# Attention's first pair of heads: one head prepared alone, the other in the first slot, with one rotation table

## The chip, the cores and the metric

The kernel runs on one core of one Trainium2 chip. A core has TensorE (PE in the views, its weight loads PEld), VectorE (DVE), ScalarE (ACT), GpSimd (POOL) and SyncE (SP), each with an instruction stream of its own that it works off in order; they wait for each other by semaphores. Data come from HBM by DMAs that are issued on a queue of an engine, here mostly SyncE's. The metric is the time of one execution on the device in microseconds, the median over several runs; lower is better.

## What is computed

```python
def _attn_ref(q, k, v):                      # (2, 8, 576, 64), f32
    def rotate(x):
        x1, x2 = (x[..., :half], x[..., half:])
        return np.concatenate([x1 * cos - x2 * sin, x1 * sin + x2 * cos], axis=-1)
    q_rot, k_rot = (rotate(q), rotate(k))
    scores = scale * np.matmul(q_rot, k_rot.transpose(0, 1, 3, 2))
    scores = scores - np.max(scores, axis=-1, keepdims=True)
    attn = np.exp(scores)
    attn = attn / (np.sum(attn, axis=-1, keepdims=True) + 1e-09)
    return np.matmul(attn, v)

def reference(...):
    x = attn_out.transpose(0, 2, 1, 3).reshape(B * S, H * D)
    x = _moe_ref(x=x, ...)       # soft mixture: 8 experts, every token through each
    return _moe2_ref(x=x, ...)   # hard mixture: a greedy assignment, 144 tokens an expert
```

Sixteen (batch, head) attentions are followed by two mixtures of experts. The change touches the start of attention alone.

## The kernel before

Attention works head after head, g = 0 to 15, two heads to a pair P. A head's rotated q and k are split into a high and a low part (`hl`, the high part rounded to the matmul's f32r format and the low part what is left), so that products keep f32 accuracy. The order of every instruction is written out by hand: each engine gets its instructions in the order in which the Python code calls them. In the loop over g (a slot for each head) the calls are collected by `at(t, f, ...)` and sorted by t, a position within the slot from 0 to 5; the table `SC` holds most positions.

Before the first slot the first pair is prepared, both heads together:

- `load` (L1127) issues for each of k, q, v three DMAs on SyncE's queue: 128 KB for each of the two heads, then 32 KB that hold the last 64 rows of both (the rest load). The tiles `rawk`, `rawq`, `rawv` are single, so the next pair's load waits until the rotation has read them. ScalarE's queue loads the rotation table `tab` in two parts of 320 KB: part 1 for k, part 0, which is part 1 scaled by 1/8, for q.
- `prep_rot` (L1176) rotates: two cross products into scratch (L1185, L1186), a product with the cosine into `t1k` or `t1q` (L1188), and the sum (L1189). For the first pair VectorE does all of k and L1188 and L1189 of q; for later pairs GpSimd does everything. `t1k` and `t1q` are single tiles.
- `prep_hl` (L1192) makes the parts: the high part on ScalarE (L1201), the low part (L1202) on VectorE for the first pair and on GpSimd later. k needs each part twice. For the first pair ScalarE and VectorE compute the second copy (L1207, L1208); later pairs get it by two DMAs inside SBUF, on SyncE's queue, 320 KB each (L1204 the high part, L1205 the low).
- `tq` (L1224) transposes a head's parts on TensorE into one PSUM bank at a time (u = 0 high k, 1 low k, 2 q, 3 the last 64 rows), and VectorE or ScalarE move them to `khh`, `kll`, `qs`. `score` (L1254) multiplies them, VectorE takes the maximum (L1264), ScalarE the exponential (L1268). `te` (L1272) transposes the exponentials, ScalarE and VectorE split them into `ah` and `al` (L1295, L1303), `pv` (L1309) multiplies with v. `prep_v` (L1210) splits v on GpSimd, two operations.
- `warm` (L1159) issues matmuls of zeros that nothing reads; the seven counts in `WARM` say how many stand at which place.

The transposes of head g+2 stand ahead of their slot: `tq(2, 0)`, the first that needs the second pair's k, stands at position 3.21 of slot 0, `tq(2, 1)` at 0.8 of slot 1, `tq(2, 2)` at 2.12 of slot 1. TensorE works in order, so whatever one of them waits for holds up all that follows.

Of the kernel before, what the change touches and what calls it, by code (L numbers as in the profile page):

```python
# [1109 lines left out]
def attention(tc, nc, ps, pss, lp, q, k, v, rope, ident, xH, xL, m1):  # L1110
    with ExitStack() as st:
# [13 lines left out]

        def load(P, names):
            if P >= B * NH // 2:  # L1127
                return
            b, pr = divmod(P, 4)
            for n in names:  # L1130
                src = SRC[n]
                t = raw[n][P % NR]
                off = (b * NH + 2 * pr) * S * HD
                for h in range(2):
                    nc.sync.dma_start(
                        t[:, h, 0:4, :].rearrange("p (t r) d -> p t (r d)", r=2),
                        bass.AP(tensor=src.tensor, offset=src.offset + off + h * S * HD,
                                ap=[[2 * HD, 128], [256 * HD, 2], [1, 2 * HD]]))
                nc.sync.dma_start(
                    t[0:64, :, 4, :],  # L1140
                    bass.AP(tensor=src.tensor, offset=src.offset + off + 512 * HD,
                            ap=[[HD, 64], [S * HD, 2], [1, HD]]))
# [33 lines left out]
        def prep_rot(P, n):  # L1176
            e1 = nc.vector if P == 0 and n == "k" else nc.gpsimd
            e2 = nc.gpsimd if P else nc.vector
            x = raw[n][P % NR]
# [1 line left out]
            cos = tab[:, ti, :, 0:64].unsqueeze(1).to_broadcast([128, 2, 5, 64])
            nsin = tab[:, ti, :, 64:96].unsqueeze(1).to_broadcast([128, 2, 5, 32])
            sin = tab[:, ti, :, 96:128].unsqueeze(1).to_broadcast([128, 2, 5, 32])
            t2 = pone.tile([128, 2, 5, HD], F32, name="t2")
            e1.tensor_tensor(t2[:, :, :, 0:32], x[:, :, :, 32:64], nsin, op=OP.mult)  # L1185
# [340 lines left out]
```

## Time and profile before

| what | value |
| --- | --- |
| time, median of 3 runs | 1189.12 us (1187.91 to 1190.19) |
| the profiled execution: its time | 1186.11 us |
| its span, first to last instruction | 1184.3 us |
| TensorE busy | 1151.8 us, 97% of the span |
| VectorE, ScalarE, GpSimd busy | 788.0, 415.8, 475.8 us |
| mean granted clock of TensorE | 0.991 of full |

The span is cut into 40 slices on the profile's page; the first, up to 29.6 us, is where the change lies. TensorE is busy for seven tenths of it and for nine tenths of most later ones. Busy time says little about the start, where TensorE also works off warm-up matmuls: there the timelines of single engines are read, an instruction a line, and the order of the instructions beside them.

### The profile page before, as it was taken

What the parts mean: (1) busy time and instruction counts of PE and PEld (TensorE: products, weight loads), DVE (VectorE), ACT (ScalarE), POOL (GpSimd) and SP (SyncE); (2) the same over time, 40 slices, a digit from 0 to 9 for tenths busy, and PEclk for the clock granted to TensorE, in tenths of its full rate; (3) what the DMA queues carried; (4) which work ended last, traced back from release to release, by engine and by line L of the source; (5) the groups of instructions that cost most, each with busy time, mean ns of one, the idle gap of its engine ahead of it and who ended that gap; (6) DMA issues with size and microseconds to landing.
All of it is one profiled execution on the core that took longest, in us unless ns stands there. A gap on an engine that the chain in (4) does not pass through costs nothing. (4 is left out here: it accounts for less than half of the span.)

```text
span 1184.3 us, 19903 instructions
## 1 busy us (share of the span) xinstructions
PE 1151.8 (97%) x7743; PEld 1036.9 (88%) x7743; DVE 788.0 (67%) x1710; ACT 415.8 (35%) x934; POOL 475.8 (40%) x428
## 2 busy tenths in 40 slices
PE   7999999999899999999999999999999999899997
PEld 4988988898798989898889898988988887899997
DVE  6999995255666666666666666548798768789200
ACT  4888886214333232323232323231121120222222
POOL 6787855405454335433543454151040000364111
PEclk8999999999899999999999999999999999999999
DMA  3223214200121112111211121142000003878830
GB/s 105 73 71 88 53 33 149 72 1 1 36 58 50 36 37 69 39 37 36 69 39 36 37 72 36 36 178 72 1 36 1 27 1 125 285 265 291 269 102 20
DMA packets 92766, 90.07 MB, mean 76 GB/s; under 512 B 26369, under 2 KB 65409, under 8 KB 92545
## 3 DMA queue, kind: packets, MB, share of 16 engines
q1 hardware_dynamic: 90336, 83.43, 22.4%
q0 software_dynamic: 2048, 4.72, 1.3%
q8 instruction: 61, 1.00, 0.4%
q10 hardware_dynamic: 288, 0.66, 0.2%
q14 instruction: 33, 0.26, 0.1%
HBM read 79.48 MB, written 4.72 MB: 71 GB/s over the span
## 5 line engine op out<-in xcount | busy, mean ns | idle before, releaser
L874 DVE TENSOR_TENSOR v<-T,v 128x256 f32<-128x256 f32 (+1 forms) x200 | 90.6, 453 | 75.9 <-PE T L861 74.6
L921 DVE SCALAR_TENSOR_TENSOR acc<-Y,pw,acc 128x512 f32<-128x512 f32 x180 | 132.3, 744 | 5.4 <-PE Y L919 2.6
L682 PE MATMUL T<-xH,wa 128*128 128x384 f32 x480 | 132.4, 337 | 0.0
L861 PE MATMUL T<-xH,wa 128*128 128x256 f32 (+1 forms) x480 | 115.4, 296 | 0.0
L861 PEld LDWEIGHTS T<-big,wb 128*128 128x128 f32 x720 | 104.4, 188 | 10.3 <-DVE v L874 3.3
L861 PE MATMUL T<-big,wb 128*128 128x256 f32 (+1 forms) x720 | 108.4, 294 | 3.1 <-DVE v L874 3.1
L701 PE MATMUL Y<-wb,hh 128*128 128x512 f32 x312 | 98.2, 396 | 1.6 <-ACT acc L708 1.6
L690 ACT ACTIVATE hh<-T 128x384 fp32r<-128x384 f32 x62 | 30.5, 492 | 185.4 <-PE T L682 185.2
L682 PEld LDWEIGHTS T<-xH,wa 128*128 128x128 f32 x480 | 87.6, 188 | 2.9
L861 PEld LDWEIGHTS T<-xH,wa 128*128 128x128 f32 x480 | 84.4, 190 | 5.1
L691 DVE SCALAR_TENSOR_TENSOR hl<-T,hh 128x384 fp32r<-128x384 f32 x62 | 34.5, 556 | 78.1 <-ACT hh L690 78.0
L682 PE MATMUL T<-xL,wa 128*128 128x384 f32 x240 | 80.6, 336 | 0.0
L861 PE MATMUL T<-xL,wa 128*128 128x256 f32 (+1 forms) x240 | 71.0, 296 | 0.0
L868 DVE SCALAR_TENSOR_TENSOR hlB<-v,hhB 128x320 fp32r<-128x320 f32 x60 | 47.4, 791 | 32.3 <-ACT hhB L867 32.3
L770 POOL TENSOR_TENSOR wa<-wraw,wa 128x512 fp32r<-128x512 f32 (+1 forms) x40 | 41.0, 1025 | 64.7 <-ACT wa L769 64.7
L701 PEld LDWEIGHTS Y<-wb,hh 128*128 128x128 f32 x312 | 57.1, 188 | 11.3 <-ACT acc L708 2.1
L789 POOL TENSOR_TENSOR wb<-wraw,wb 128x512 fp32r<-128x512 f32 x20 | 25.5, 1296 | 99.8 <-ACT wb L788 99.8
L867 ACT ACTIVATE hhB<-v 128x320 fp32r<-128x320 f32 x60 | 28.3, 472 | 104.2 <-DVE v L874 104.2
L789 POOL TENSOR_TENSOR wa<-wraw,wa 128x512 fp32r<-128x512 f32 x20 | 25.9, 1318 | 96.2 <-ACT wa L788 96.2
L1264 DVE TENSOR_REDUCE negmax<-S 128x1 f32<-128x576 f32 (+1 forms) x80 | 60.1, 752 | 5.5 <-PE S L1262 4.7
L919 PE MATMUL Y<-wa,hhB 128*128 128x512 f32 x200 | 62.9, 396 | 0.0
L919 PE MATMUL Y<-wb,hhB 128*128 128x512 f32 x200 | 62.8, 396 | 0.0
(292 smaller groups left out, 3041.8 us busy)
## 6 DMA issues: line engine op xcount, KB each, us to landing
wraw<-in_moe_w SPq DMA_DIRECT2D x56, 512.0 KB, 5.0
big<-in_moe_w SPq DMA_DIRECT2D x22, 512.0 KB, 6.3
wraw<-in_moe_w SPq DMA_DIRECT2D x40, 256.0 KB, 3.2
wa<-in_moe_w SPq DMA_DIRECT2D x18, 512.0 KB, 5.1
wb<-in_moe_w SPq DMA_DIRECT2D x12, 512.0 KB, 5.9
hlk<-hlk SPq DMA_DIRECT2D x14, 320.0 KB, 3.4
ysc<-acc SPq DMA_DIRECT2D x9, 256.0 KB, 2.1
rawk<-in_k SPq DMA_DIRECT2D x16, 128.0 KB, 3.9
```

What stands on the lines that cost most here:

```text
L682: nc.tensor.matmul(p[:, :CH], w[:, wi, kt, (fb % 2) * 128:(fb % 2) * 128 + 128], x[:, kt, o], start=(n == 0), stop=(n == 11))
L690: nc.scalar.activation(hh, p[:, :CH], AF.Relu)
L691: nc.vector.scalar_tensor_tensor(hl, p[:, :CH], 0.0, hh.bitcast(F32), op0=OP.max, op1=OP.subtract)
L701: nc.tensor.matmul(self.Y[c][t], a[:, o], w[:, wi, fb % 2], start=(fb == 0 and n == 0), stop=(fb == FB - 1 and n == 2))
L770: G.tensor_tensor(l, src, h.bitcast(F32), op=OP.subtract)
L789: G.tensor_tensor(d["W"][:, 1, h], r[:, 2 + h], d["W"][:, 0, h].bitcast(F32), op=OP.subtract)
L861: nc.tensor.matmul(bank[:, 0:n], d[t][:, ww, b, r * 128:(r + 1) * 128], x(xw, r), start=(first and i == 0), stop=(i == 5), skip_group_chec ...
L868: V.scalar_tensor_tensor(HL[:, f, o], src, 0.0, HH[:, f, o].bitcast(F32), op0=OP.max, op1=OP.subtract)
L874: V.tensor_tensor(o, bank[:, 0:n], x, op=OP.add)
L919: nc.tensor.matmul(y, h[:, f, o], w[:, ww, f], start=(f == 0 and z == 0), stop=(f == 1 and z == 2))
L921: V.scalar_tensor_tensor(self.acc[:, t], y, self.pw[:, t, e:e + 1], self.acc[:, t], op0=OP.mult, op1=OP.add)
L1264: nc.vector.tensor_reduce(m[0:n], p[0:n, :, :288], axis=AX.XY, op=OP.max, negate=True)
```

## The change

Only head 0 of the first pair is loaded first (k, its rest, q, its rest), rotated and split before the first slot; head 1 follows inside slot 0. k's first head is rotated on VectorE, q's first head and k's second head on GpSimd, q's second head on VectorE in slot 0. The scratch tile is one for k and one for q. One rotation table is loaded; ScalarE computes the scaled one from it. The rotation of the next pair's k and q moves into slot 0, behind the first pair's second head and on either side of `prep_v`; its `prep_hl` moves from positions 0.9 (k) and 2.9 (q) of slot 0 to 3.1 of slot 0 and 1.6 of slot 1; the load of pair 2's k and q moves from 0.9 to 3.1. `tq(1, 0)` and `tq(1, 1)` move from positions 0.01 and 0.02 to 2.05 and 2.06; `tq(1, 2)` and `tq(1, 3)` stay at 2.12 and 2.16. The counts of warm-up matmuls at the first three places go from 8, 6, 3 to 16, 3, 2.

```diff
-        WARM = (8, 6, 3, 4, 3, 2, 2)
+        WARM = (16, 3, 2, 4, 3, 2, 2)
...
-        load(0, "k")
-        nc.scalar.dma_start(tab[:, 1], rope[:, 1])
-        load(0, "q")
-        nc.scalar.dma_start(tab[:, 0], rope[:, 0])
+        nc.scalar.dma_start(tab[:, 1], rope)
+        for n in "kq":
+            load_h(0, n, 0)
+            load_r(0, n)
+        for n in "kq":
+            load_h(0, n, 1)
         load(0, "v")
+        nc.scalar.activation(tab[:, 0], tab[:, 1], AF.Copy, scale=0.125)
...
-        def prep_rot(P, n):
-            e1 = nc.vector if P == 0 and n == "k" else nc.gpsimd
-            e2 = nc.gpsimd if P else nc.vector
-            x = raw[n][P % NR]
+        def prep_rot(P, n, h=None, e=nc.gpsimd):
+            hs = slice(0, 2) if h is None else slice(h, h + 1)
+            nh = hs.stop - hs.start
+            x = raw[n][P % NR][:, hs]
...
-            t2 = pone.tile([128, 2, 5, HD], F32, name="t2")
+            t2 = pone.tile([128, 2, 5, HD], F32, name="t2" + n)[:, hs]
...
+            if not h:
+                T1[n, P] = pone.tile([128, 2, 5, HD], F32, name="t1" + n)
+            t1 = T1[n, P][:, hs]
+            e.tensor_tensor(t1, x, cos, op=OP.mult)
+            e.tensor_tensor(t1, t1, t2, op=OP.add)
...
-        prep_rot(0, "k")
-        prep_rot(0, "q")
-        load(1, "kq")
-        prep_hl(0, "k")
-        prep_hl(0, "q")
+        prep_rot(0, "k", 0, nc.vector)
+        prep_rot(0, "q", 0)
+        prep_hl(0, "k", 0)
+        prep_rot(0, "k", 1)
+        load(1, "k")
+        prep_hl(0, "q", 0)
...
-        prep_rot(1, "k")
-        prep_rot(1, "q")
...
-                        at(SC["tqs"] + 0.01 * u, tq, 1, u)
+                        at(2.05 + 0.01 * u, tq, 1, u)
...
-                at(0.9, prep_hl, 1, "k")
-                at(0.9, load, 2, "kq")
+                at(0.02, prep_rot, 0, "q", 1, nc.vector)
+                at(0.02, load, 1, "q")
+                at(0.9, prep_hl, 0, "k", 1)
+                at(0.91, prep_rot, 1, "k")
+                at(1.3, prep_hl, 0, "q", 1)
                 at(1.9, prep_v, 0)
                 at(1.9, load, 1, "v")
-                at(2.9, prep_hl, 1, "q")
+                at(1.92, prep_rot, 1, "q")
+                at(3.1, prep_hl, 1, "k")
+                at(3.1, load, 2, "kq")
+            if g == 1:
+                at(1.6, prep_hl, 1, "q")
```

`prep_hl` gets the same parameter h. The host makes one table instead of two. The lines of the changed kernel lie some 10 to 15 higher: L1196, L1197, L1201, L1202 are the four operations of a rotation, L1216 and L1222 the low parts, L1228 and L1229 `prep_v`, L1130 and L1139 the loads, L1218 and L1219 the two copies.

GpSimd, from the rotation of the second pair's k on; before (big_113 is the split v, the names with numbers are scratch):

```order
L1185 TENSOR_TENSOR t_207<-rawk_96,tab 128x10x32 [waits DMAHW4_49,DMAHW3_49,DMAHW5_49,DMAHW0_49,DVE_49]
L1186 TENSOR_TENSOR t_207<-rawk_96,tab 128x10x32
L1188 TENSOR_TENSOR t1k<-rawk_96,tab 128x640 [waits DVE_49]
L1189 TENSOR_TENSOR t1k<-t1k,t_207 128x640 [waits Pool_49]
L1185 TENSOR_TENSOR t_213<-rawq_95,tab 128x10x32 [waits DMAHW6_49,DMAHW7_49,DMAHW0_49,Pool_49]
L1186 TENSOR_TENSOR t_213<-rawq_95,tab 128x10x32
L1188 TENSOR_TENSOR t1q<-rawq_95,tab 128x640 [waits DVE_49]
L1189 TENSOR_TENSOR t1q<-t1q,t_213 128x640 [waits Pool_49]
L1202 TENSOR_TENSOR hlk<-t1k,hlk 128x10x64 [waits Activation_49]
L1214 TENSOR_TENSOR big_113<-rawv_97,zero 128x2x5x64 [waits DMAHW2_49,DMAHW1_49]
L1215 TENSOR_TENSOR big_113<-rawv_97,big_113 128x2x5x64 [waits Pool_49]
L1202 TENSOR_TENSOR hlq<-t1q,hlq 128x10x64 [waits Activation_49]
```

The same place in the changed kernel, from the last operation on the first pair's second k head:

```order
L1202 TENSOR_TENSOR t1k<-t1k,t2k 128x320 [waits Pool_49]
L1196 TENSOR_TENSOR t2k<-rawk_96,tab 128x10x32 [waits DMAHW3_49,DMAHW4_49,DMAHW2_49,Pool_49]
L1197 TENSOR_TENSOR t2k<-rawk_96,tab 128x10x32
L1201 TENSOR_TENSOR t1k<-rawk_96,tab 128x640 [waits DVE_49]
L1202 TENSOR_TENSOR t1k<-t1k,t2k 128x640 [waits Pool_49]
L1228 TENSOR_TENSOR big_113<-rawv_97,zero 128x2x5x64 [waits DMAHW7_49,DMAHW1_49,DMAHW0_49]
L1229 TENSOR_TENSOR big_113<-rawv_97,big_113 128x2x5x64 [waits Pool_49]
L1196 TENSOR_TENSOR t2q<-rawq_95,tab 128x10x32 [waits DMAHW7_49,DMAHW6_49,DMAHW5_49]
L1197 TENSOR_TENSOR t2q<-rawq_95,tab 128x10x32
L1201 TENSOR_TENSOR t1q<-rawq_95,tab 128x640 [waits DVE_49]
L1202 TENSOR_TENSOR t1q<-t1q,t2q 128x640 [waits Pool_49]
L1216 TENSOR_TENSOR hlk<-t1k,hlk 128x10x64 [waits Activation_49]
```

The split of v has come ahead of q's rotation and q's rotation ahead of k's low part, and the third operation of k's rotation has a wait for VectorE.

SyncE's queue, from the second pair's k load on; before:

```order
L1135 DMA rawk_96<-in_k 128x2x128 [waits DMAHW3_49,DVE_49]
L1135 DMA rawk_96<-in_k 128x2x128 [waits DMAHW4_49]
L1139 DMA rawk_96<-in_k 64x2x64 [waits DMAHW5_49]
L1135 DMA rawq_95<-in_q 128x2x128 [waits DMAHW6_49,DVE_49,Pool_49]
L1135 DMA rawq_95<-in_q 128x2x128 [waits DMAHW7_49]
L1139 DMA rawq_95<-in_q 64x2x64 [waits DMAHW0_49]
L1204 DMA hlk<-hlk 128x10x64 [waits DMAHW1_49,Activation_49]
L1205 DMA hlk<-hlk 128x10x64 [waits DMAHW2_49,Pool_49]
L1135 DMA rawk_96<-in_k 128x2x128 [waits DMAHW3_49]
L1135 DMA rawk_96<-in_k 128x2x128 [waits DMAHW4_49]
L1139 DMA rawk_96<-in_k 64x2x64 [waits DMAHW5_49]
L1135 DMA rawq_95<-in_q 128x2x128 [waits DMAHW6_49]
```

And in the changed kernel:

```order
L1130 DMA rawk_96<-in_k 128x2x128 [waits DMAHW2_49,DVE_49]
L1130 DMA rawk_96<-in_k 128x2x128 [waits DMAHW5_49,DMAHW3_49,Pool_49]
L1139 DMA rawk_96<-in_k 64x2x64 [waits DMAHW4_49]
L1130 DMA rawq_95<-in_q 128x2x128
L1130 DMA rawq_95<-in_q 128x2x128 [waits DMAHW6_49,DVE_49]
L1139 DMA rawq_95<-in_q 64x2x64 [waits DMAHW7_49]
L1130 DMA rawv_97<-in_v 128x2x128 [waits DMAHW0_49,Pool_49]
L1130 DMA rawv_97<-in_v 128x2x128 [waits DMAHW1_49]
L1139 DMA rawv_97<-in_v 64x2x64 [waits DMAHW2_49]
L1218 DMA hlk<-hlk 128x10x64 [waits DMAHW3_49,Activation_49]
L1219 DMA hlk<-hlk 128x10x64 [waits DMAHW4_49,Pool_49]
```

The second pair's v load, which stood behind the two hlk copies and the third pair's loads, stands ahead of the copies, with its wait for GpSimd.

VectorE, from the first pair's low parts to the first low part of weights (al); before:

```order
L1202 TENSOR_TENSOR hlk<-t1k,hlk 128x10x64 [waits Activation_49]
L1208 TENSOR_TENSOR hlk<-t1k,hlk 128x10x64 [waits Activation_49]
L1202 TENSOR_TENSOR hlq<-t1q,hlq 128x10x64 [waits Activation_49]
L1244 CAST khh<-T 128x512 [waits PE_49]
L1244 CAST kll<-T 128x512 [waits PE_49]
L1251 CAST kll<-T 128x64 [waits Activation_49]
L1264 TENSOR_REDUCE negmax<-S 128x1 [waits PE_49] x2
L1244 CAST khh<-T 128x512 [waits PE_49]
L1244 CAST kll<-T 128x512 [waits PE_49]
L1264 TENSOR_REDUCE negmax<-S 128x1 [waits PE_49]
L1303 SCALAR_TENSOR_TENSOR al<-T,ah 128x4x128 [waits Activation_49]
```

In the changed kernel, from the first two maxima on:

```order
L1278 TENSOR_REDUCE negmax<-S 128x1 [waits PE_49] x2
L1196 TENSOR_TENSOR t2q<-rawq_95,tab 128x5x32 [waits DMAHW6_49,DMAHW4_49]
L1197 TENSOR_TENSOR t2q<-rawq_95,tab 128x5x32
L1201 TENSOR_TENSOR t1q<-rawq_95,tab 128x320
L1202 TENSOR_TENSOR t1q<-t1q,t2q 128x320 [waits DVE_49]
L1278 TENSOR_REDUCE negmax<-S 128x1 [waits PE_49]
L1317 SCALAR_TENSOR_TENSOR al<-T,ah 128x4x128 [waits Activation_49]
L1216 TENSOR_TENSOR hlk<-t1k,hlk 128x5x64 [waits Activation_49]
L1222 TENSOR_TENSOR hlk<-t1k,hlk 128x5x64 [waits Activation_49]
L1278 TENSOR_REDUCE negmax<-S 128x1 [waits PE_49]
L1317 SCALAR_TENSOR_TENSOR al<-T,ah 128x4x128 [waits Activation_49]
L1216 TENSOR_TENSOR hlq<-t1q,hlq 128x5x64 [waits DVE_49,Activation_49]
```

q's second head is rotated between the second and the third maximum, and three half low parts stand behind the scores instead of in front of them.

## Rows read from the trace of the kernel before

**Rows 1.** Stage table: stretch, length, busy us (count) of each engine, PEclk, DMA, GB/s

```profile
1.27:4.90 3.63, 3.59 (x8) 1.01 (x8) 0.47 (x7) 1.28 (x1) 0.54 (x4) 1.00 0.81 245
...
8.00:9.00 1.00, 0.00 (x0) 0.00 (x0) 0.97 (x3) 0.02 (x1) 0.00 (x0) 0.86 0.00 0
10.45:15.00 4.55, 4.38 (x14) 2.33 (x14) 3.75 (x4) 0.74 (x1) 3.61 (x4) 0.50 0.26 73
15.00:16.00 1.00, 0.71 (x5) 0.33 (x4) 1.00 (x2) 0.00 (x0) 1.00 (x1) 0.73 0.00 0
...
40.00:60.00 20.00, 19.94 (x155) 17.85 (x153) 18.11 (x34) 17.53 (x44) 15.34 (x12) 1.00 0.30 79
```

**Rows 2.** DMA issues at 0.75, 0.76, 1.76, 8.11, 21.62, 25.11: count, KB, us to landing

```profile
tab<-const_rope ACTq DMA_DIRECT2D x1, 320.0 KB, 3.6
...
rawk<-in_k SPq DMA_DIRECT2D x1, 128.0 KB, 3.8
...
rawk<-in_k SPq DMA_DIRECT2D x1, 32.0 KB, 4.6
...
rawk<-in_k SPq DMA_DIRECT2D x1, 128.0 KB, 2.2
...
hlk<-hlk SPq DMA_DIRECT2D x1, 320.0 KB, 3.2
...
hlk<-hlk SPq DMA_DIRECT2D x1, 320.0 KB, 3.4
```

**Rows 3.** Timeline of VectorE, 6 to 19: start, us, line, operation, count [idle before]

```profile
6.46 0.49 DVE L1185 TENSOR_TENSOR t<-rawk,tab 128x320 f32<-128x320 f32 x1 [4.72 <-DMA rawk<-in_k]
...
8.12 0.82 DVE L1189 TENSOR_TENSOR t1k<-t1k,t 128x640 f32<-128x640 f32 x1
...
14.13 1.48 DVE L1202 TENSOR_TENSOR hlq<-t1q,hlq 128x640 fp32r<-128x640 f32 x1
...
17.99 1.42 DVE L1264 TENSOR_REDUCE negmax<-S 128x1 f32<-128x576 f32 x2 [0.66 <-PE S L1262]
```

**Rows 4.** Timeline of GpSimd, 13 to 28

```profile
13.49 1.44 POOL L1186 TENSOR_TENSOR t<-rawk,tab 128x320 f32<-128x320 f32 x1
...
18.74 0.85 POOL L1185 TENSOR_TENSOR t<-rawq,tab 128x320 f32<-128x320 f32 x1
...
23.52 1.56 POOL L1202 TENSOR_TENSOR hlk<-t1k,hlk 128x640 fp32r<-128x640 f32 x1
...
26.37 1.56 POOL L1215 TENSOR_TENSOR big<-rawv,big 128x640 fp32r<-128x640 f32 x1
```

**Rows 5.** Timeline of TensorE, 10 to 36

```profile
10.48 1.09 PE L1222 MATMUL T<-ident,hlk 128*128 128x128 f32 x4 [5.62 <-ACT hlk L1207]
...
15.67 0.66 PE L1222 MATMUL T<-ident,hlq 128*128 128x128 f32 x4 [0.28 <-DVE hlq L1202]
...
17.07 0.62 PE L1260 MATMUL S<-khh,qs 128*128 128x288 f32 x2
...
26.47 0.51 PE L1260 MATMUL S<-khh,qs 128*128 128x288 f32 x2
...
27.09 0.60 PE L1222 MATMUL T<-ident,hlk 128*128 128x128 f32 x4
...
31.19 0.60 PE L1222 MATMUL T<-ident,hlk 128*128 128x128 f32 x4
31.63 0.60 PE L1222 MATMUL T<-ident,big 128*128 128x128 f32 x4
...
34.21 0.60 PE L1222 MATMUL T<-ident,hlq 128*128 128x128 f32 x4
```

**Rows 6.** Timeline of ScalarE, 6 to 10

```profile
8.98 0.74 ACT L1201 ACTIVATE hlk<-t1k 128x640 fp32r<-128x640 f32 x1 [6.00 <-DVE t1k L1189]
```

**Rows 7.** Timeline of the SyncE queue, 8 to 10

```profile
8.11 0.89 SPq L1135 DMA_DIRECT2D rawk<-in_k  x2
9.04 0.61 SPq L1139 DMA_DIRECT2D rawk<-in_k  x1
```

More of the change, by code (lines that the diff above doesn't have):

```diff
@@ L1124, in attention, with load_h, load_r @@
         SRC = {"k": k, "q": q, "v": v}
+        def load_h(P, n, h):
+            b, pr = divmod(P, 4)
+            src = SRC[n]
+            off = (b * NH + 2 * pr) * S * HD
+            nc.sync.dma_start(
+                raw[n][P % NR][:, h, 0:4, :].rearrange("p (t r) d -> p t (r d)", r=2),
+                bass.AP(tensor=src.tensor, offset=src.offset + off + h * S * HD,
+                        ap=[[2 * HD, 128], [256 * HD, 2], [1, 2 * HD]]))
+        def load_r(P, n):
+            b, pr = divmod(P, 4)
+            src = SRC[n]
+            off = (b * NH + 2 * pr) * S * HD
+            nc.sync.dma_start(
+                raw[n][P % NR][0:64, :, 4, :],
+                bass.AP(tensor=src.tensor, offset=src.offset + off + 512 * HD,
+                        ap=[[HD, 64], [S * HD, 2], [1, HD]]))
         def load(P, names):
@@ L1128, in load @@
                 return
-            b, pr = divmod(P, 4)
             for n in names:
-                src = SRC[n]
-                t = raw[n][P % NR]
-                off = (b * NH + 2 * pr) * S * HD
                 for h in range(2):
[L1135 to L1142, printed above, removed]
+                    load_h(P, n, h)
+                load_r(P, n)
         for n in "kqv":
@@ L1174, in attention, with prep_hl @@
         T1 = {}
[L1176 to L1179 removed]
+        def prep_rot(P, n, h=None, e=nc.gpsimd):
+            hs = slice(0, 2) if h is None else slice(h, h + 1)
+            nh = hs.stop - hs.start
+            x = raw[n][P % NR][:, hs]
             ti = 0 if n == "q" else 1
[L1181 to L1196 removed]
+            cos = tab[:, ti, :, 0:64].unsqueeze(1).to_broadcast([128, nh, 5, 64])
+            nsin = tab[:, ti, :, 64:96].unsqueeze(1).to_broadcast([128, nh, 5, 32])
+            sin = tab[:, ti, :, 96:128].unsqueeze(1).to_broadcast([128, nh, 5, 32])
+            t2 = pone.tile([128, 2, 5, HD], F32, name="t2" + n)[:, hs]
+            e.tensor_tensor(t2[:, :, :, 0:32], x[:, :, :, 32:64], nsin, op=OP.mult)
+            e.tensor_tensor(t2[:, :, :, 32:64], x[:, :, :, 0:32], sin, op=OP.mult)
+            if not h:
[3 more added lines that the diff above has]
+            e.tensor_tensor(t1, t1, t2, op=OP.add)
+        def prep_hl(P, n, h=None):
+            dup = 2 if n == "k" else 1
+            if not h:
+                HL[n, P] = ptwo.tile([128, 2, 5, 2, dup, HD], F32R, name="hl" + n)
+            hs = slice(0, 2) if h is None else slice(h, h + 1)
+            t1 = T1[n, P][:, hs]
+            hl = HL[n, P][:, hs]
             xr = t1.rearrange("p h j d -> p (h j) d")
@@ L1475, in host_consts @@
     tok = token_order()
-    rope = np.zeros((128, 2, 5, 128), np.float32)
-    for i, sc in enumerate((np.float32(0.125), np.float32(1.0))):
-        for j in range(5):
-            n = 128 if j < 4 else 64
-            s = tok[j * 128:j * 128 + n]
-            rope[:n, i, j, 0:32] = cos[s] * sc
-            rope[:n, i, j, 32:64] = cos[s] * sc
-            rope[:n, i, j, 64:96] = -sin[s] * sc
-            rope[:n, i, j, 96:128] = sin[s] * sc
+    rope = np.zeros((128, 5, 128), np.float32)
+    for j in range(5):
+        n = 128 if j < 4 else 64
+        s = tok[j * 128:j * 128 + n]
+        rope[:n, j, 0:32] = cos[s]
+        rope[:n, j, 32:64] = cos[s]
+        rope[:n, j, 64:96] = -sin[s]
+        rope[:n, j, 96:128] = sin[s]
     rt = np.zeros((128, 328), np.float32)
```

9 lines of the change are left out of this document (removed).

## The prediction

> **What bounds the kernel now.** I read the stage table first. In the long attention stretch TensorE is busy 19.94 of 20 us [rows 1], so from there on a delay of TensorE is a delay of the kernel, and an early start is worth what is left of it when that stretch is reached. Before it there is a preparation of some 17 us that TensorE mostly spends on warm-up matmuls. The timeline of VectorE shows what it waits for: 4.72 us of idling until a piece of k has landed, the rotation from 6.46 to 8.94, the last low part (q) from 14.13 to 15.61 [rows 3]. TensorE then transposes q at 15.67 and scores at 17.07 [rows 5]; the first score is 1.46 us behind the last low part. The third view is the one that decides, TensorE again: at 27.09 it transposes the second pair's k high part, at 31.19 the k low part, at 34.21 the q of that pair [rows 5]. These need copies that SyncE makes inside SBUF, which land 3.2 and 3.4 us after their issue [rows 2]. In the kernel before they are there over 2 us ahead; the reader should watch them, not the start.
>
> **Part 1, the loads and the start.** The k rest load is issued third now, at 1.76, and lands 4.6 us later, at 6.36; the first head's 128 KB lands 3.8 us after 0.76, and the table 3.6 us after 0.75 [rows 2]. After the change the rest is second, at about 1.2. It lands no earlier than the head in front of it (4.6) and no later than 1.2 + 4.6 = 5.8. I take 1.2 + 3.8 = 5.0, by the head's row, which is next to it in the queue. Half rotations: 320 elements take 0.49 us, 640 take 0.82 [rows 3], so 160 take an estimated 0.33; four half operations lie between half of the present 2.48 us and 0.33 + 0.33 + 0.49 + 0.49 = 1.64; 1.5 taken, end 6.5. Two ScalarE halves, between 0.37 and 0.74 each [rows 6], 0.42 taken: TensorE could start at 7.4 where it starts at 10.48 now [rows 5]. Sixteen warm-ups, eight of which take 3.59 us from 1.27 [rows 1], last to 8.4 at the half clock; they cover this and cost nothing, for q is later. The second table is now a ScalarE copy (about 0.74, as its 640-wide row [rows 6]), done by 5.1 while q's first head lands at about 6.0: hidden.
>
> q's first head goes to GpSimd: four half operations, half of 0.85, 0.85, 1.56 and 1.56 [rows 4], 2.4 us, and 0.5 more where VectorE works beside it: 6.0 to 9.0. ScalarE 0.42, VectorE's low part 0.5 to 0.9: 10.3. First score at 10.3 + 1.46 = 11.8, against 17.07. **The front gains 5.3 us.**
>
> **Part 2, the second head in the first slot.** What left the preparation comes back behind the first scores. VectorE: first maximum 0.92 after the first score, two maxima 1.42 [rows 3, 5] (14.1); then q's second head, 1.64 alone, 2.3 taken because GpSimd works beside it (a 640-wide operation of VectorE takes 1.48 there instead of 0.82, GpSimd's 320-wide one 1.44 instead of 0.85 [rows 3, 4]); a maximum and a low part of weights, 0.7 each; then two half low parts of k's second head, 0.5 each: 18.8. The Trainium skill, SBUF — State Buffer, section "SBUF: two separate sides", says that VectorE with two SBUF inputs and GpSimd take the common port for whole instructions, the loser blocked. The rows agree in kind; by that rule alone a short VectorE half could wait out a 1.56 us operation, and the sum would come an estimated 0.7 us later.
>
> By itself this still leaves TensorE ahead: the second head's first score, now at 26.47 [rows 5], would come at 22 to 23, some 4 us early.
>
> **Part 3, the second pair, where I expect the loss.** Several edits meet here.
>
> (a) GpSimd now rotates k's second head first: 9.0 to 11.8, its third operation done at 10.9. Only then may the load of the next pair's k second head be issued (the buffer is single): 0.46 and 0.61 of issue [rows 7] and 2.2 us of landing [rows 2] make 13.7. The two cross products of the next k take 1.7 alone and 2.8 beside VectorE: 16.2 at most. Its third operation writes t1k, which is single too and is read until VectorE's half low parts end at 18.8. So the wait is on VectorE's first slot, a new one. 18.8 + 3.1 (two 640-wide ones of 1.56 [rows 4]) = 22.0, where the rotation now is over by 18.74.
>
> (b) v comes next on GpSimd instead of q. Its two operations take from the end of the low part before them (23.52 + 1.56) to 26.37 + 1.56, 2.85 us [rows 4]: until 24.9. On SyncE the load of the next v has moved ahead of the two copies, and it waits for this; its three issues take 1.5 [rows 7], so the first copy is issued at 26.4 and lands 3.2 later, at **29.6**. TensorE wants it at 22 to 23 and got it, before, in time for 27.09: **2.5 us late against before**, with the front's gain gone.
>
> (c) q's rotation now stands ahead of k's low part on GpSimd: 4.8 us (18.74 to 23.52) and 1.56 [rows 4], 24.9 to 31.3; the second copy lands 3.4 later at **34.7**, against 31.19: **3.5 us late**. Bounds: with all GpSimd operations alone and VectorE done by 17.4 it lands at 33.1 (1.9 late); with one more lengthening of VectorE's first slot by the 0.66 us of rows 3 at 35.4 (4.2 late).
>
> (d) q's low part has moved into the second slot. Behind the k low transposes come a group of transposes (31.63 after 31.19, 0.44 later), its drain 0.6, ScalarE's eviction 0.6 and q's high part 0.74, GpSimd's 1.56: 3.9 us where TensorE needs 3.02 (31.19 to 34.21) [rows 5]: **0.9 more**.
>
> (e) TensorE idles from about 23 to 29.6. The idle in the trace to compare it with is the one after the first warm-ups: they end at 4.9, the granted clock falls in the slice 8 to 9, and comes back from 0.50 (1.2 GHz) between 15 and 16, some 4.9 us after work resumed at 10.48 [rows 1, 5]. Here it would be at half from about 27 to 34.5. Between the two copies there are 5.1 us for work that takes 4.1 now with its gaps; about 2.5 us of it would be done by 34.5 and 1 to 1.6 is left. Between 0 (the clock holds) and 1.7; 1.0 taken. The Trainium skill, TensorE: Matmul & The Clock Gate, section "HAM oscillation — how this bites in real kernels", names just this, an idle stretch that throttles the next work; the rows above agree.
>
> Sum: 3.5 + 0.9 + 1.0 = **5.4 us later**. The rest of attention has TensorE busy throughout [rows 1], so nothing gives it back, and the later stages follow attention without a fixed start. On the profiled execution 1186.1 + 5.4 = 1191.5; that execution is 3.0 below the median shown (1189.1), and the forecast is made for the median: **1194.5 us**.
>
> **Rivals.**
> 1. *The copies come in time* (faster). Then the 4 us lead of the first slot stays: 1185.1. It decides at one point: GpSimd's v must end by 23 - 3.2 - 1.5 = 18.3. Against it: everything alone and no wait for VectorE gives 6.0 + 2.4 + 1.7 = 10.1 for the third operation, 12.8 with the load (0.46 + 2.2), 17.6 after the rotation (4.8), 20.5 after v. For it: only an order on the queues that I have misread, or q landing 2 us earlier.
> 2. *GpSimd is not slowed and the clock holds*: the low bound, 1.9 + 0.9, less about 1 us that TensorE would make up because ScalarE and VectorE have caught up while it waited: 1.8 later, 1190.9, within 0.2%. For it: the 4.1 us between its two uses of the copies hold gaps that are waits for those two; against: the slowing is there to be read [rows 3, 4], and the clock did fall after such an idle stretch [rows 1].
> 3. *The loads don't do what they should*: the two queues share what moves the bytes, and if removing a table brings nothing, the rest lands at 5.8 and q's first head at 7. Everything in part 3 hangs on these, so the loss grows by 0.8 to 1.5: 1195.7.
>
> **How the numbers follow.** About 0.2% (2.4 us) is what a measurement here can tell from no change. Forecast 0.70, rival 1 0.08, rival 2 0.14, rival 3 0.08. So faster 0.08, same 0.14, slower 0.78. The range goes from just under rival 2 (1190.0) to the upper bound with the whole clock term, 4.2 + 0.9 + 1.7 = 6.8 (1195.9), and rival 3's 1.5 on it with some for what its late loads do to the first slot: 1198.0.
>
> **What would show it.** Right: first score at 11 to 13; GpSimd's third operation on the next k waits for VectorE; SyncE's next v load waits for GpSimd's v; TensorE idles 5 us or more before a transposition of hlk near 30, and again short of 35, with the clock at 0.50 around it; the slots after that keep their length. Wrong: the hlk transposes run without an idle ahead of them, or the second slot begins under 29 us, or the first score stays above 15 (then part 1 has failed).

## The result

The changed kernel takes 1196.54 us (median; 1193.83 to 1197.37 in five runs) where the kernel before takes 1189.12: 1.0066 of it, 95% interval 1.0049 to 1.0083. It is slower by 7.4 us. The kernel before stands here with five runs, 1187.81 to 1190.19; the ratio goes by all runs and need not be the quotient of the two medians (1.0062). The forecast was 1194.5, range 1190.0 to 1198.0. Executions of one and the same kernel spread over 2.3 to 8.6 us here, so small differences below are read from landmarks in the traces and not from times.

The first view is TensorE's timeline of the changed kernel (start, us, line, operation, count, idle before), the rows that answer to [rows 5]:

```profile
7.58 0.60 PE L1236 MATMUL T<-ident,hlk 128*128 128x128 f32 x4
...
12.02 0.52 PE L1274 MATMUL S<-khh,qs 128*128 128x288 f32 x2
...
22.72 0.51 PE L1274 MATMUL S<-khh,qs 128*128 128x288 f32 x2
...
29.56 1.09 PE L1236 MATMUL T<-ident,hlk 128*128 128x128 f32 x4 [6.07 <-DMA hlk<-hlk]
...
35.45 0.60 PE L1236 MATMUL T<-ident,hlk 128*128 128x128 f32 x4
...
39.46 0.66 PE L1236 MATMUL T<-ident,hlq 128*128 128x128 f32 x4 [0.83 <-POOL hlq L1216]
...
49.64 0.63 PE L1236 MATMUL T<-ident,rcp 128*128 128x128 f32 x4 [0.75 <-DVE al L1317]
```

The first transposes come at 7.58 instead of 10.48 and the first score at 12.02 instead of 17.07. The second head is still 3.75 us ahead (22.72 against 26.47). Then TensorE idles 6.07 us for a copy of the second pair's k: 29.56 against 27.09, 35.45 against 31.19, 39.46 against 34.21. Why the copies are late stands in GpSimd's timeline and in the SyncE queue's:

```profile
18.36 1.54 POOL L1201 TENSOR_TENSOR t1k<-rawk,tab 128x640 f32<-128x640 f32 x1 [1.42 <-DVE hlk L1222]
...
22.95 1.55 POOL L1229 TENSOR_TENSOR big<-rawv,big 128x640 fp32r<-128x640 f32 x1
...
27.69 1.53 POOL L1202 TENSOR_TENSOR t1q<-t1q,t2q 128x640 f32<-128x640 f32 x1
29.18 1.53 POOL L1216 TENSOR_TENSOR hlk<-t1k,hlk 128x640 fp32r<-128x640 f32 x1
37.86 1.55 POOL L1216 TENSOR_TENSOR hlq<-t1q,hlq 128x640 fp32r<-128x640 f32 x1 [7.14 <-ACT hlq L1215]
```

```profile
24.53 0.89 SPq L1130 DMA_DIRECT2D rawv<-in_v  x2
25.46 0.61 SPq L1139 DMA_DIRECT2D rawv<-in_v  x1
26.17 0.64 SPq L1218 DMA_DIRECT2D hlk<-hlk  x1
30.74 0.62 SPq L1219 DMA_DIRECT2D hlk<-hlk  x1
```

GpSimd waits for VectorE before its third operation on the next k, splits v (until 24.50), rotates q, and only then splits k. SyncE's next v load waits for the v split and is issued ahead of the first copy. Last, the stage table (columns as in [rows 1]), with one stretch from the routing stage at its end:

```profile
24.00:26.00 2.00, 0.00 (x0) 0.00 (x0) 0.29 (x1) 1.43 (x4) 2.00 (x3) 1.00 0.15 45
26.00:28.00 2.00, 0.00 (x0) 0.00 (x0) 0.00 (x0) 0.00 (x0) 1.92 (x3) 0.88 0.60 159
28.00:30.00 2.00, 0.44 (x2) 0.47 (x3) 0.00 (x0) 0.00 (x0) 2.00 (x2) 0.50 0.40 107
...
32.00:34.00 2.00, 2.00 (x12) 1.98 (x11) 1.16 (x2) 0.48 (x1) 0.00 (x0) 0.50 0.87 215
34.00:36.00 2.00, 2.00 (x17) 2.00 (x16) 1.71 (x3) 1.50 (x5) 0.00 (x0) 0.91 0.70 191
40.00:60.00 20.00, 19.25 (x149) 17.25 (x148) 17.50 (x31) 16.63 (x41) 16.30 (x14) 1.00 0.31 78
...
1018.00:1026.00 8.00, 7.03 (x54) 6.77 (x55) 6.11 (x20) 2.30 (x5) 1.11 (x1) 0.50 0.91 316
```

The clock falls to 0.50 in the idle and is back only between 34 and 36. In the stretch 40 to 60 TensorE is as busy as before but for 0.7 us [rows 1]. VectorE's last row maximum of the attention, the landmark used below, starts at 192.29 instead of 186.27: **6.0 us of attention**. The distance of the two traces then stays at 6.0 to 6.1 for more than 700 us. In the routing stage, from 970 us on, another 4.4 come in this pair of executions; the section on that stage says where these are from.

### The profile page after: what moved, and what is told of

Its sections match the earlier page's. It is cut to its first block, busy times and chain, and to the rows that moved or that the text cites. A ratio compares the mean times of both kernels' runs of the same rounds, so it can differ in the third digit from the quotient of the medians.

```text
span 1194.8 us, 19922 instructions
## 1 busy us (share of the span) xinstructions
PE 1158.4 (97%) x7747; PEld 1042.2 (87%) x7747; DVE 788.7 (66%) x1715; ACT 417.8 (35%) x938; POOL 476.2 (40%) x434
```

## The experiments

Theory at the start: the loss is the second pair's chain, that is, the order on GpSimd and SyncE, one single buffer, and the clock after the idle. Rivals: the work added to VectorE in the first slots, the loads, or the clock alone. "Gather" below is the time from the issue of the last result block's write (SyncE, ysc) to GpSimd's first gather of expert rows, which must wait for that write. Each ratio is to the runs of the kernel before that were made together with the kernel's own (medians 1188.79 for e1 to e4, 1189.31 for e6, e7, e9 and e10, 1190.09 for f1 to f4), so that times of different groups are compared with care.

| kernel | last row maximum | gather | median us | ratio to before, 95% |
| --- | --- | --- | --- | --- |
| before | 186.27 | 5.34 | 1189.12 | 1 |
| changed | 192.29 | 5.47 | 1196.54 | 1.0066 [1.0049, 1.0083] |
| changed, again (e9) | 193.43 | 5.57 | 1195.11 | 1.0052 [1.0037, 1.0066] |
| e1 v load later | 190.98 | 5.53 | 1194.52 | 1.0048 [1.0031, 1.0065] |
| e2 own t1 | 196.20 | 5.74 | 1195.50 | 1.0051 [1.0034, 1.0068] |
| e3 large filler | 190.61 | **3.31** | 1189.15 | 1.0013 [1.0000, 1.0026] |
| e4 k before q | 189.20 | 5.57 | 1191.08 | 1.0016 [1.0003, 1.0029] |
| e10 engines write both | 189.56 | 5.53 | 1190.69 | 1.0012 [1.0001, 1.0023] |
| f2 changed + 24 small | 193.56 | **3.32** | 1192.06 | 1.0030 [1.0011, 1.0049] |
| f3 short chain + 24 small | 187.77 | **3.14** | 1185.51 | 0.9968 [0.9952, 0.9985] |
| e6 before, one table | 186.97 | 5.31 | 1187.92 | 0.9988 [0.9970, 1.0007] |
| e7 before + 28 large | 191.05 | **3.25** | 1189.07 | 1.0005 [0.9992, 1.0018] |
| f4 before + 128 small | 188.73 | 4.92 | 1192.20 | 1.0024 [1.0008, 1.0040] |
| f1 before + 28 small | 186.11 | **3.28** | 1184.76 | 0.9968 [0.9948, 0.9987] |

### e4: k's split ahead of q's rotation

```
 at(1.9, prep_v, 0)
-at(1.9, load, 1, "v")
-at(1.92, prep_rot, 1, "q")
-at(3.1, prep_hl, 1, "k")
+at(2.5, prep_hl, 1, "k")
+at(2.51, load, 1, "v")
+at(2.52, prep_rot, 1, "q")
```

> The changed kernel with one thing reordered: the second pair's k split stands ahead of the second pair's q rotation on GpSimd, and its two copies stand ahead of the next v load on SyncE. All instructions are the same. Theory (the loss is the order of GpSimd and SyncE in the second pair's chain): the k rotation still ends near 21.7 us, the high part follows on ScalarE near 22.9 to 23.6, so the first copy issues near 23.7 instead of 26.17 and the first transposes of the second pair start near 27.0 instead of 29.56; the low part runs behind v, 24.5 to 26.0, so the second copy issues near 26.1 instead of 30.74 and its transposes start near 31 instead of 35.45. The last row maximum of the attention comes at 187 +-1 us instead of 192.29 (before: 186.27), and the time is 5 us +-1.5 under the changed kernel's, 1191 to 1192. Rival (VectorE's and GpSimd's added work in the first two slots, or the loads, cost the time): the order gives back under 2 us of attention, and the time stays above 1194.

TensorE's timeline of e4, the two groups that wait for the copies:

```profile
26.18 1.09 PE L1236 MATMUL T<-ident,hlk 128*128 128x128 f32 x4 [3.43 <-DMA hlk<-hlk]
...
32.38 0.60 PE L1236 MATMUL T<-ident,hlk 128*128 128x128 f32 x4
```

Three lines of order give back 3.1 of the 6.0 us of attention, 0.8 of it by an earlier first score in this execution (11.26 instead of 12.02) and 2.3 by the order. That is the theory's mechanism and not its size: the first copy comes 3.4 us earlier, of which again 0.8 is the earlier start, but TensorE still idles 3.43 for it, and the second group stands at 32.38 and not at 31, with no wait named: the half clock holds it up.

### e1: the v load behind the copies

```
-at(1.9, load, 1, "v")
...
+at(3.1, load, 1, "v")
 at(3.1, load, 2, "kq")
```

> The changed kernel with one thing moved: the next v load stands behind the second pair's two copies on SyncE. Theory (each late copy costs its own lateness): the high part is ready near 24.7 us, so the first copy issues near 24.8 instead of 26.17 and the transposes that wait for it start near 28.1 instead of 29.56; the second copy still issues near 30.7 behind GpSimd's q rotation, so it bounds the rest, and the last row maximum of the attention comes 0.5 to 1.4 us earlier than 192.29. Rival (the first copy alone decides, the second is hidden): all of the 1.4 us reaches the last row maximum. Rival (SyncE's order has no part in it): nothing moves. Time 1195.5 +-1.2.

```profile
27.93 1.09 PE L1236 MATMUL T<-ident,hlk 128*128 128x128 f32 x4 [4.62 <-DMA hlk<-hlk]
...
34.18 0.63 PE L1236 MATMUL T<-ident,hlk 128*128 128x128 f32 x4
```

The first group moves by 1.63, the second by 1.27, the last maximum by 1.31; 0.2 of each is an earlier first score (11.82). The rival that the first copy alone decides is nearer: most of it arrives, though the second copy is issued as late as before (30.56). So in the changed kernel the second copy was not what held TensorE at 35.45; the work at half clock was.

### e3: filler against the clock

```
+at(3.205, warm, 24)
```

> The changed kernel with 24 more zero matmuls of 512 columns on TensorE in the 6.07 us of idle ahead of the second pair's first transposes (24 x 0.21 us = 5.1 us at the full clock). They use no result. Theory: the transposes still start near 29.6 us, for the copy sets that; the granted clock holds at 0.9 or more over 28 to 34 us instead of 0.50, the work between the two copies shortens by 1 to 2 us until the second copy (landing near 34) bounds it, and the last row maximum of the attention comes 0.7 to 1.5 us earlier than 192.29; time 1195.5 +-1.2. Rival (the half clock is nearly all of the loss): the last row maximum comes 3 us earlier or more. Rival (the work at half clock hides behind the second copy): under 0.4 us.

e3's stage table and TensorE's timeline:

```profile
28.00:30.00 2.00, 1.16 (x10) 0.80 (x9) 0.31 (x1) 0.00 (x0) 2.00 (x2) 1.00 0.20 52
30.00:32.00 2.00, 2.00 (x18) 1.90 (x17) 2.00 (x5) 1.14 (x3) 0.22 (x1) 1.00 0.19 51
```

```profile
29.03 0.63 PE L1236 MATMUL T<-ident,hlk 128*128 128x128 f32 x4 [0.84 <-DMA hlk<-hlk]
...
33.87 0.63 PE L1236 MATMUL T<-ident,hlk 128*128 128x128 f32 x4 [0.92 <-DMA hlk<-hlk]
```

With the clock at 1.00 throughout, the first group comes as late as ever, and now the second copy does bind (0.92 idle). Counted from the first score, the second group is at 22.37 instead of 23.43: the clock's price is **1.06 us**, net of what the second copy then holds up. The last maximum gains 1.68, of which 0.5 is an earlier first score (11.50). But the time fell by 7.4 us against the changed kernel's first runs and by 6.0 against its ten later ones (e9), about four times that. The rest is in the routing stage (below).

### e2: no wait for VectorE

```
+if (P, n, h) == (0, "k", 1):
+    t1 = T1["x"] = pone.tile([128, 1, 5, HD], F32, name="t1x")
```

(and the split of that head reads it.)

> The changed kernel with a tile of its own for the rotated second head of the first pair's k, so that GpSimd's rotation of the second pair's k does not wait for VectorE's split of that head (1.42 us of wait before the op at 18.36 us). Theory: GpSimd's whole queue behind it comes 1.4 us earlier (k rotation ends near 20.3, v near 23.1, q near 27.8, k low part near 29.3), the copies issue near 24.8 and 29.4, the last row maximum of the attention comes 1.4 to 2.0 us earlier than 192.29, and the time is near 1194.9 (+-1.2). Rival (the wait is no part of the loss): GpSimd waits for something else in its place and the last row maximum moves by less than 0.4 us.

The opposite happened: the last maximum came 3.9 us later. First VectorE in the changed kernel, then VectorE, GpSimd and TensorE in e2:

```profile
15.17 1.05 DVE L1202 TENSOR_TENSOR t1q<-t1q,t2q 128x320 f32<-128x320 f32 x1
...
17.80 0.48 DVE L1222 TENSOR_TENSOR hlk<-t1k,hlk 128x320 fp32r<-128x320 f32 x1
...
46.28 0.84 DVE L1337 TENSOR_SCALAR den<-sum 128x10 f32<-128x10 f32 x1
```

```profile
16.78 1.73 DVE L1204 TENSOR_TENSOR t1q<-t1q,t2q 128x320 f32<-128x320 f32 x1
...
20.17 1.53 DVE L1224 TENSOR_TENSOR hlk<-t1x,hlk 128x320 fp32r<-128x320 f32 x1
```

```profile
16.35 1.81 POOL L1203 TENSOR_TENSOR t1k<-rawk,tab 128x640 f32<-128x640 f32 x1
...
19.86 1.50 POOL L1230 TENSOR_TENSOR big<-rawv,zero 128x640 fp32r<-128x640 f32 x1
```

```profile
20.10 0.66 PE L1238 MATMUL T<-ident,big 128*128 128x128 f32 x4 [2.06 <-ACT big L1284]
...
23.12 1.08 PE L1238 MATMUL T<-ident,hlk 128*128 128x128 f32 x4 [1.94 <-DVE al L1319]
```

Freed of its wait, GpSimd went straight on to its 640-wide operations. The end of VectorE's rotation of q beside the first of them took 1.73 us instead of 1.05, and the second half low part of k beside a later one 1.53 instead of 0.48; each ends shortly after GpSimd's operation does. TensorE idled 2.06 and 1.94 us, its clock stood at 0.50 already over 22 to 28, and the second pair followed late. The wait was a cover: the half low parts ran in 0.47 and 0.48 us while GpSimd stood still. (The Trainium skill, SBUF — State Buffer, section "SBUF: two separate sides", states an exclusive lock between the two; these rows agree.) Not all of the 3.9 us is the wait's: e2's first slot also has a longer form that executions with the wait have too (see e9), and against those, e9 and f2, its last maximum is 2.6 to 2.8 us later.

### e10: no copies in the second pair's chain

```
-at(3.1, prep_hl, 1, "k")
+at(2.5, k1_high)
...
+at(3.28, k1_low)
...
-at(1.6, prep_hl, 1, "q")
+at(1.3, prep_hl, 1, "q")
```

(k1_high is two copies on ScalarE, k1_low two subtractions on VectorE; v load and q rotation as in e4.)

> The changed kernel with three edits to the second pair: both copies of k's high part are written by ScalarE (2 x 0.73 us) behind the v split, and both of its low part by VectorE (0.8 to 1.5 us each) where it idles, so no DMA copy stands in that pair's chain; the next v load follows on SyncE without a copy ahead; q's split moves from 1.6 to 1.3 in its slot. Theory (the second pair's chain is the whole loss, and the front's 5 us are kept where it is short): the first transposes of the second pair start near 23.6 to 24.3 us instead of 29.56, the next near 29, q's near 33, the granted clock stays at 0.9 or more over 22 to 36 us, the last row maximum of the attention comes at 181 to 183 us (before: 186.27), and the time is 4 us +-2 under the kernel before. Rival (the front's gain does not carry, since GpSimd's queue of q's rotation and split is late next): q's transposes start near 35 and the last row maximum comes at 184 to 186, and the time is within 2 us of the kernel before.

e10's VectorE and TensorE:

```profile
26.84 2.91 DVE L1233 TENSOR_TENSOR hlk<-t1k,hlk 128x640 fp32r<-128x640 f32 x2
...
44.21 0.16 DVE L1349 TENSOR_SCALAR den<-sum 128x10 f32<-128x10 f32 x1
```

```profile
30.97 0.63 PE L1248 MATMUL T<-ident,hlk 128*128 128x128 f32 x4 [2.00 <-DVE al L1329]
...
35.80 0.66 PE L1248 MATMUL T<-ident,hlq 128*128 128x128 f32 x4 [1.45 <-POOL hlq L1216]
```

The long idle is gone (first group at 24.95), and two shorter ones stand in its place: 2.00 us behind VectorE, whose two low parts take 2.91, and 1.45 for q. The rival is nearer: the next link was late, with q at 35.80 and the time 1.4 us over the kernel before. But the last maximum, at 189.56, is later than either had it.

### e9 and e6: the spread, and the table alone

e9 is the changed kernel without an edit.

> The changed kernel once more, without an edit, for the spread: the last row maximum of the attention between 191.5 and 193 us, the time near 1196 (+-1.2). The stretch from the last row maximum to the last matmul was 994.9 us in the one execution shown and 987.4 to 994.9 in the others; theory: it differs from execution to execution with the granted clock past 970 us, and not by the kernel.

Its last maximum is 1.1 us later than in the first execution (just outside what was expected), most of it because the second head's first transposes stand 7.2 us behind the first score and not 6.3. Of the eight traces with this first slot four have 6.3 (changed, e1, e3, e4) and four 7.0 to 7.2 (e9, e10, f2, f3). VectorE's and GpSimd's timelines show the difference. In the four with 6.3, GpSimd's rotation of the next k, which waits for a load, starts no earlier than VectorE's third operation on q (14.81 against 14.65 in the changed kernel). In e10, f2 and f3 it starts before that (14.56 against 14.74 in e10), and one or two of VectorE's short operations take 0.99 to 1.16 us instead of 0.32 and 0.48. In e9 the clock was at 0.50 over 12 to 14, and VectorE's rotation of q began 3.0 us behind the first score instead of 2.2. The attention's loss is therefore 6.0 to 7.3 us by execution.

e6 is the kernel before with `tab[:, 0]` made by ScalarE from one table.

> The kernel before with one part of the change alone: one rotation table of 328 KB is loaded instead of two, and ScalarE scales it by 0.125 for q. Theory: k's rotation waits for k and its own table and not for the second one, so the first score moves by 0 to 1 us from 17.07, the attention's last row maximum by 0 to -1 us from 186.27, and the time is within 1.2 us of the kernel before. Rival (the loads are what the front gained by): the first score comes 2 us earlier or more.

k's rotation starts 0.86 us earlier (5.60), but the first score does not (17.26), and the time is the same within its interval. The smaller table alone is not the front's gain; the loads of one head at a time, the other half of that rival, no run tests by themselves.

### The routing stage: e7, f1, f4, f2

e7 is the kernel before with a delay:

```
+if g == 4:
+    at(0.05, warm, 28)
```

> The kernel before with 28 zero matmuls of 512 columns (28 x 0.21 = 6.0 us at the full clock) ahead of the fifth head's first transposes, and nothing else. They use no result. Theory (the attention is bounded by TensorE from there on, and what happens past it is a shift): the last row maximum comes 6.0 us +-0.3 later than 186.27, and the time is 6 us +-1.2 over the kernel before: what the changed kernel pays over its 6.0 us in the attention is then the spread of the late stage. Rival (a shift of that size itself costs more in the routing stage): 7.5 us or more.

Both were wrong: the last maximum came 4.8 us later and the time stayed where it was. e7 and e3, the two kernels with added large matmuls, share something else. In the changed kernel's trace the gather's row numbers (ix), the last write, the gather and TensorE's first use of it are:

```profile
1002.48 0.16 DVE L328 SCALAR_TENSOR_TENSOR ix<-idf 72x4 int32<-72x4 f32 x1
...
1009.30 0.34 SPq L951 DMA_DIRECT2D ysc<-acc  x1
...
1014.77 1.15 POOL L338 DMA_INDIRECT xa<-ysc,ix  x1 [19.86 <-DVE u L282]
...
1018.06 0.38 PE L413 MATMUL Y<-ident,xa 72*128 72x72 f32 x1 [3.00 <-DMA xa<-ysc,ix]
```

and in e3 (the instruction queue of the window 1004.5 to 1005, GpSimd, TensorE):

```profile
q8 instruction: 1, 0.02, 12.3%
...
1009.56 1.15 POOL L338 DMA_INDIRECT xa<-ysc,ix  x1 [17.70 <-DVE cmp L232]
...
1012.80 0.28 PE L413 MATMUL Y<-ident,xa 72*128 72x72 f32 x1 [0.79 <-DMA xa<-ysc,ix]
```

The view names VectorE as what released the gather, but its row numbers had been there since 1002.64; what was still to come was the write. The write of e3 was issued at 1006.25, so its gather follows 3.3 us later, not 5.5, and TensorE waits 0.79 instead of 3.00; after the longer wait the changed kernel ran eight us at 0.50 (table above), e3 did not. The DMA queues of the changed kernel, 1010 to 1011 and 1011 to 1013 (packets, MB, share):

```profile
q1 hardware_dynamic: 135, 0.25, 65.1%
q8 instruction: 1, 0.02, 10.0%
...
q1 hardware_dynamic: 9, 0.02, 3.4%
```

A load of instructions falls among the 144 packets of the last write, and 9 of these come 1 to 2 us after the others. The load is one packet of 16 KB; its 10.0% of 16 engines' microsecond is 1.6 us on one of them. Packet by packet the trace has it from 1010.39 to 1011.99, and the 9 follow one behind the other from 1011.98 to 1013.00. Nine is 144 / 16 (eight of the 128 packets of 2 KB and one of the 16 of 4 bytes): one DMA engine's share of the write, which waited until that engine had finished the load. The trace does not name the engine, but in all nine traces with a late gather the first of 9 late packets starts within 0.03 us of the load's end, and the gather starts 1.5 to 1.8 us after the write's last packet in all fourteen. In e3 the load lies 1.5 us ahead of the write and all 144 are through in 1 us. The page tells whose instructions they are likely to be:

```profile
PE 1158.4 (97%) x7747; PEld 1042.2 (87%) x7747; DVE 788.7 (66%) x1715; ACT 417.8 (35%) x938; POOL 476.2 (40%) x434
...
q8 instruction: 61, 1.00, 0.4%
```

7747 matmuls and as many weight loads in 61 packets of 16 KB: 254 instructions each. (The Trainium skill, Runtime: NRT & Kernel Launch, section "Instruction fetch mechanics", gives 16 KB blocks of 256 instructions and calls the cost of crossing from one to the next mostly hidden; the count agrees, and what shows here is a cost to another transfer.) That gives a test: the number of TensorE's instructions should decide, and 256 more should change nothing. The added lines of f1 (kernel before, behind the first warm-ups), f4 (kernel before, fifth head, where e7 has its 28) and f2 (changed kernel, first slot); each tiny matmul has 8 columns:

```
+tiny(28)
...
+at(0.05, tiny, 128)
...
+at(3.205, tiny, 24)
```

> The kernel before with 28 zero matmuls of 8 columns on TensorE in its idle time ahead of the first transposes (idle from 4.9 to 10.48 us); they use no result. Theory (in the profiles so far the gather of the first expert's rows starts 5.3 to 5.7 us after the last result block's write is issued where an instruction-load packet falls 0.75 to 1.0 us behind that issue, and 3.3 us after it in the two kernels with 24 and 28 more matmuls, where the packet falls 1.5 us ahead of it; the packets follow TensorE's instruction count): the packet moves ahead of the write, the gather starts near 3.3 us after the issue, TensorE waits near 0.8 us instead of 2.76 for it, the clock does not fall there, the last row maximum stays within 0.6 us of 186.27, and the time comes 3 to 6 us under the kernel before. Rival (the shift in time made it, not the count of instructions): the gather stays at 5.3 us or more and the time within 1.2 us of the kernel before.

> The kernel before with 128 zero matmuls of 8 columns ahead of the fifth head's first transposes: 256 more instructions of TensorE, as many as one load packet carries by the page (61 packets for 2 x 7747 instructions is 254 each), at the place where the kernel with 28 large ones had them. They use no result. Theory (the phase of the packets decides): the packets fall again where they fell before, the gather starts 5.3 us or more after the last write's issue, the attention is 3 to 5 us longer, and the time is 3 to 6 us over the kernel before. Rival (any delay or added work there removes the wait): the gather starts near 3.3 us and the time is within 1.5 us of the kernel before, as with the 28 large ones.

> The changed kernel with 24 zero matmuls of 8 columns (under 1 us in all) in TensorE's 6 us of idle ahead of the second pair's transposes: as many instructions as the 24 large ones had, and too little work to hold the clock. They use no result. Theory: the attention stays as in the changed kernel (last row maximum 192 to 193.5 us), the gather starts near 3.3 us after the last write's issue, the clock does not fall there, and the time is 3 to 6 us under the changed kernel's, near 1191, and 5 to 7 us over the kernel before with 28 small ones: the change's own cost, with the same late stage on both sides. Rival (the 24 large ones gained by the clock alone): the time stays above 1194.5.

f1: load 1.5 us ahead of the write, gather at 3.28, attention unmoved, and the time 0.9968 of the kernel before: 3.8 us gained by the ratio, 5.3 by the medians, by 28 matmuls that compute nothing. f4, with 256 instructions more, has a 62nd packet on that queue; its load is back at 1.07 us behind the issue, the gather at 4.92 (this load took 1.14 us, the shortest of the nine), and the time is over that of before by 2.1 to 2.9, which is what its attention lost (2.5); gather, attention and time are all less than I expected. In all fourteen traces of the table the gather is 4.9 us or more where the load falls in the write (nine) and under 3.4 where it does not (five). From the last row maximum to the end, the nine take 998.0 to 1002.5 us and four of the five 995.0 to 996.7; the fifth, f1's trace, is an execution with the clock low all the same (1002.1, see the end).

f2 against f1 compares the change with the same late stage on both sides: 1192.06 - 1184.76 = 7.3 us (I had expected 5 to 7), with 7.45 between their last maxima. **So the change's own loss is all in the attention.** The 4.4 us of the routing stage in the first pair of traces belong to executions: in both the load hit the write, but the clock was low for longer in one (0.83 against 1.00 over 970 to 980, where 1.6 us of it arise; 0.87 and 0.62 over 1010 to 1020 and 1020 to 1030, against 0.83 and 1.00).

### f3: everything together

```
+at(2.5, k1_high)
+at(2.51, k1_low)
+at(2.51, load, 1, "v")
+at(2.52, prep_rot, 1, "q")
...
+at(3.205, tiny, 24)
+at(4.36, k1_low2)
...
+at(1.3, prep_hl, 1, "q")
```

Here k1_low is one subtraction on GpSimd behind v, and k1_low2 a copy of it on ScalarE.

> The changed kernel with the second pair's chain cut short and the instruction phase moved: ScalarE writes both copies of k's high part and the second copy of its low part, GpSimd the low part itself right behind v and ahead of q's rotation, no DMA copy in that pair; q's split at 1.3 instead of 1.6 in its slot; 24 zero matmuls of 8 columns that use no result. Theory: the second pair's first transposes start near 25 us, the next near 29 (31 where VectorE wrote both low parts), q's near 33 to 34, the last row maximum comes at 184 to 186.5 us (before: 186.27), the gather starts near 3.3 us after the last write's issue, and the time is 4 to 7 us under the kernel before, the best of all. Rival (GpSimd's queue is too long for the second pair whatever the order): q's transposes start after 35 us, the last row maximum comes after 188, and the time is no better than that of the kernel before with 28 small matmuls.

```profile
24.95 0.66 PE L1258 MATMUL T<-ident,hlk 128*128 128x128 f32 x4
...
28.82 0.60 PE L1258 MATMUL T<-ident,hlk 128*128 128x128 f32 x4
...
34.04 0.98 PE L1258 MATMUL T<-ident,hlq 128*128 128x128 f32 x4 [1.83 <-POOL hlq L1221]
```

No wait is left ahead of either k group, but q is 1.83 us late and the clock falls again; the last maximum is 1.5 us behind that of before, between theory and rival; in time the rival is right. Two comparisons with the late stage alike tell what the chain is worth. Against f2, the changed kernel with the same 24 matmuls, f3's shorter chain gives back 5.8 us of attention (187.77 against 193.56) and 6.6 of the medians. **So most of the change's 7.3 to 7.45 us was the second pair's chain**, and the work that the change adds to VectorE in the first slots, which f3 keeps, is not the loss: behind it TensorE is still ahead (the second head's first score at 23.49, in f1 at 26.32). What is left against f1 is 1.7 us (186.11), behind the wait for q. But against f1, the kernel before with the same phase of instruction loads, f3 gains nothing (1184.76 and 1185.51, intervals alike): over the kernel before itself it is ahead by that phase alone.

## Why the prediction was right

- **Front gain 5.3**: 5.05. Rival 3 (the loads) falls: first score 12.02, forecast 11.8.
- **(a) the new wait**: forecast third operation of GpSimd at 18.8, rotation done at 22.0; 18.36 and 21.66. The wait is there, 1.42 us, for VectorE's half low part (17.80 + 0.48). Two sums ahead of it don't come out: 10.9 + 0.46 + 0.61 + 2.2 is 14.2 and not 13.7, and with 2.8 for the cross products 17.0 and not 16.2. Measured are 14.81 and 16.93; nothing hung on them, as VectorE came last.
- **(b) first copy**: v until 24.9, issue 26.4, TensorE 29.6; measured 24.50, 26.17, 29.56. Rival 1 needed v by 18.3.
- **(c) and (e), second copy and clock**: 3.5 + 1.0 = 4.5 late; 4.26. The copy would have let TensorE go near 34.4 (issued 30.74, and e3's was used 3.6 us after its issue), 3.2 late, and the work at half clock took until 35.45; e3 gives the clock term as 1.06. The second idle that the prediction names short of 35 is not there: the work at half clock filled it, as its own reckoning in (e) implies.
- **(d) q's split**: 0.9 forecast, 5.25 - 4.26 = 0.99 measured.
- **What was missing**: 0.8 us between q's group and the last maximum. At 49.64 TensorE waits 0.75 for VectorE, whose 10-element operation at 46.28 took 0.84 us; in e10 it took 0.16 and that wait is not there. GpSimd's queue, still late, was running beside it in the changed kernel, with an operation from 45.51 to 47.08; in e10 and in the kernel before GpSimd's next one starts just behind it. No run changes this alone. So the sum of 5.4 became 6.0, and with the longer form of the first slot up to 7.3: the forecast is 2 us short of the first five runs and 0.6 of e9's ten, inside its range.
- **The median**: adding the sum to the median of before was right, as f1 and f2 show, though neither trace of the first pair would have told so: their routing stages differ by 4.4 us for another reason. That both stood alike there was luck: the prediction has no term for where instruction loads fall, and the change adds only 4 matmuls, where 24 to 28 move the load out of the write.
- **The start**: 16 warm-ups were to last to 8.4 "at the half clock"; the row cited has 1.00 there, and they took 6.47 us and ended at 7.74. Nothing hung on it.
- Rival 2 stays out: GpSimd was slowed, the clock fell. Its gain with a held clock, but a slowed GpSimd, is e3's 1.06.

Open: why the load that GpSimd waits for, and so the form of the first slot, differs between executions; and what share of f1's gain is the earlier gather and what the clock behind it.

## What to carry to other kernels

An earlier start is worth what the next piece of the pipeline can take up: before splitting the first pair, ask when the second pair's last input will be ready, and put its steps on each in-order queue ahead of work that is wanted later. Before removing a wait, see which engine works undisturbed during it. And where two kernels differ by a few us, compare the traces far from the edit as well: 24 to 28 matmuls, added at three different places, moved an instruction load more than 900 us later out of a write.

## What the hardware showed unexpectedly

- 28 matmuls of 8 columns in idle time made a kernel of 1190 us faster by 0.3%: an instruction load no longer fell into a write that a gather waits for (gather 3.3 us after the issue instead of 5.3).
- One 16 KB instruction packet took 1.14 to 1.96 us there, and a sixteenth of the write's packets, 9 of 144, came only at its end, in nine traces of nine.
- The early gather does not exclude a low clock: f1's profiled execution (1189.96 us, its slowest of twelve) had the early gather and yet 0.57 over 1010 to 1020.
- A GpSimd wait of 1.42 us, removed, cost attention instead of giving some back: 3.9 us against the first execution, 2.6 to 2.8 against the two later ones (e2).
